# Turning queries and keys by transposing DMA instead of on TensorE, in a kernel of windowed attention and an MLP

## The chip, the cores and the metric

The kernel runs on one core of one Trainium2 chip. The metric is device time in microseconds of one execution; lower is better.

## The reference

Eight batches, eight heads, 576 positions, 64 elements a head. Attention looks at the position itself and the 127 before it, with a bias that falls with distance and has a slope of its own for each head. The heads are put side by side (512 columns), normalised over the columns, and go through two matrix products with a ReLU between them; the input of the normalisation is added to the result.

```python
scores = scale * np.matmul(q, k.transpose(0, 1, 3, 2))
mask = (rel >= 0) & (rel < 128)                 # rel = query position - key position
scores = np.where(mask, scores - slopes * rel, -1e9)
attn = exp(scores - max); attn /= attn.sum(-1)
x = np.matmul(attn, v)                          # heads side by side: (8, 576, 512)
xn = (x - mean) / np.sqrt(var + 1e-6) * g_ln
out = x + np.maximum(xn @ w_ch1, 0.0) @ w_ch2   # 512 -> 2048 -> 512
```

Inputs and outputs are float32; the products run in float16 with float32 sums.

## The kernel before

Batches are taken in four pairs `p` (0 to 3). A pair has nine blocks: blocks 0 to 7 are 128 positions of one batch (block `2i + b` holds positions 128i to 128i + 127 of the pair's batch `b`), and block 8, called `T`, holds the last 64 positions of both batches. `order` lists the 36 blocks; `n` is a block's place in it, so that pairs 2 and 3 are blocks 18 to 35. Blocks are gathered into twelve groups for the MLP, six of two blocks and then six of four.

A block passes through these steps:

- `load_qk` and `load_v` bring q, k and v into SBUF with DMAs from POOL (GpSimd), which turn float32 into float16 on the way. `load_until` issues the loads in the order of `loads`, up to six blocks ahead (`AHEAD`). One `load_qk` serves two blocks (or the tail); its tile is of `raw_pool`, with four buffers for q and four for k, so that a load waits until the turn four before it has read its buffer. Row `c` of a half tile takes positions 2c and 2c + 1, that is 128 neighbouring elements of a head.
- `turn` brings the head's 64 elements onto partitions, as the scores' matmul wants them: 64 transposes of 64 x 64 on TensorE (32 for the tail, line 277) into PSUM, and copies from there to SBUF on VectorE (DVE) and ScalarE (ACT). Where `in_sc` is set they use the two pairs of banks of the scores, `ps_sc`. Queries stay in the order "even positions, then odd ones", keys are put back into natural order by the copy (lines 296 and 297). The tables of `distances`, and from them the masks, have the queries' order. The tiles are of `turned_pool`.
- `attend` (line 393) multiplies queries and keys in 64 x 64 tiles and leaves out, through `seen`, what the mask will make zero anyhow; ScalarE takes the exponential (line 401), VectorE multiplies by the mask (line 412).
- `values` multiplies by v (line 445); VectorE divides by the row sums (lines 453, 454) and so empties the PSUM bank.
- From block 8 on, `stats` makes mean and variance on VectorE (lines 542, 543) and the reciprocal deviation `rstd` with two small operations on POOL (lines 497 and 500). `normal` makes `xc` on VectorE (line 484) and turns it with a transposing DMA on SP (SyncE) into the group's `xT` (line 492).
- `mlp1` (line 677) makes the hidden layer, `mlp2` (line 710) or `fast_mlp2` (line 776, with fewer products) the output. VectorE adds x (`finish`, line 852, or `add`, line 794) and SP stores. In `finish` and `add` a PSUM bank comes free. Products and values share four PSUM banks (`ps_mm`, from the seventh group on as the list `ring`).

For TensorE, ScalarE and VectorE the order of the program is the order written (`manual_schedule`): `steps` holds for each block n the turn of block n + 3, the values of block n, the scores of block n + 2, the statistics and then `normal` of block n, and `weave_at` sets these steps between the matmuls of the MLP. For POOL and SP the order is found by the scheduler when the program is built; each engine works through its list strictly in order. A DMA on SP or POOL waits, beside its data, for the eighth DMA before it on its queue.

A store writes rows back in two DMAs, one for even and one for odd positions, except for the tails.

Of the kernel before, what the change touches and what calls it, by code (L numbers as in the profile page):

```python
# [10 lines left out]
FP16 = mybir.dt.float16  # L11
# [6 lines left out]
P = 128  # L18
# [4 lines left out]
T = 8  # L23
# [2 lines left out]
GROUPS = [2] * 6 + [4] * 6  # L26
FAST = 6

NV = 10
AHEAD = 6  # L30

FIRST_GROUPS, FIRST = 2, 4
# [6 lines left out]
def distances():  # L39

    key = np.arange(P)[:, None]
    query = np.arange(P)[None, :]

    def far(rel, ok=True):
        return np.where(ok & (rel >= 0) & (rel < WINDOW), rel, FAR)

    ends = [far(P + query - HALF * b - key, query // HALF == b) for b in range(2)]  # L50
    tail = far(query - key, query // HALF == key // HALF)
    evens_first = np.r_[0:P:2, 1:P:2]
    both = [far(P + query - key), far(query - key)]
    cols = [m[:, evens_first] for m in both] + [*ends, tail]
    return np.concatenate(cols, axis=1).astype(np.float16)


# [1 line left out]
def kernel(  # L59
# [21 lines left out]
    def pool(name, bufs, **kw):  # L81
        return ctx.enter_context(tc.tile_pool(name=name, bufs=bufs, **kw))

    consts = pool("consts", 1)
    raw_pool = pool("raw", 4)
    turned_pool = pool("turned", 3)
    probs_pool = pool("probs", 4)
    own_pool = pool("own", 2)
    x_pool = pool("x", 7)
# [34 lines left out]

    g_sb = consts.tile([P, NKB], FP32)
    nc.sync.dma_start(out=g_sb, in_=moe_g_ln.rearrange("(kb p) -> p kb", p=P))
    g_line = consts.tile([1, DM], FP32)
    nc.sync.dma_start(out=g_line, in_=moe_g_ln.rearrange("(o d) -> o d", o=1))
    g_row = consts.tile([P, DM], FP32)
    one_line = consts.tile([1, P], FP32)  # L130
    magic = consts.tile([P, 4], I32)
    ones = consts.tile([P, 4 * P], FP16)
# [3 lines left out]
    w1 = consts.tile([P, NKB, FFN], FP16)  # L136
    w1g = consts.tile([P, NKB, FFN], FP16)
    w2 = consts.tile([P, NFB, DM], FP16)
    QF, QD = NFB // 2, DM // 2
    hsum = [consts.tile([P, QF, 2 * P], FP16, name=f"hs{i}", tag=f"hs{i}") for i in range(2)]  # L140
    spare = [w1[:, i, :].rearrange("p (f d) -> p f d", d=QD) for i in range(4)]
    hsum.append(spare[3])
    vext = [
# [60 lines left out]

    raw = {}

    def load_qk(src, tag, p, i):

        n = min(P, S - i * P)
        t = raw_pool.tile([P, H, 2, D], FP16, tag=tag, name=tag)  # L210
        raw[tag, p, i] = t
        for b in range(2):
            nc.gpsimd.dma_start(  # L213
                out=t[b * n // 2 : (b + 1) * n // 2],
                in_=src[2 * p + b, :, i * P : i * P + n, :].rearrange(
                    "h (c r) d -> c h r d", r=2
                ),
            )
# [64 lines left out]
    def turn(p, i, in_sc=False, copies=(nc.vector.tensor_copy, nc.scalar.copy)):  # L283

        ps = [bank(b if in_sc else None) for b in range(2)]
        k = keys_tile("k", p, i)  # L290
        if i < 4:
            q = queries(p, i)
            transposed("q", p, i, [t[:, 0] for t in ps])
            transposed("k", p, i, [t[:, 1] for t in ps])
            for b, copy in enumerate(copies):
                copy(out=q[:, b], in_=ps[b][:, 0])  # L296
                copy(out=k[:, b].rearrange("p h (c r) -> p r h c", r=2), in_=ps[b][:, 1])  # L297
        else:
            q = keys_tile("q", p, i)
            for tag, t, dst, copy in zip("qk", ps, (q, k), copies):  # L300
                transposed(tag, p, i, [t[:, 0]])
                copy(out=dst[:, 0].rearrange("p h (c r) -> p r h c", r=2), in_=t[:, 0])

    def bank(sc=None):
        if sc is None:
            return ps_mm.tile([P, 2, 2, HP, HALF], FP16, tag="mm", name="ps_tr")
        return ps_sc[sc][:, 0].bitcast(FP16).rearrange(
            "p (t r h c) -> p t r h c", t=2, r=2, h=HP
        )

    def queries(p, i):
        t = turned_pool.tile([P, 2, 2, HP, HALF], FP16, tag="q", name="q")
        turned["q", p, i] = t.rearrange("p b r h c -> p b h r c")
        return t

    def keys_tile(tag, p, i):
        t = turned_pool.tile([P, 2, HP, P], FP16, tag=tag, name=tag)
# [2 lines left out]

    def turn_first():

        q, k = queries(0, 0), keys_tile("k", 0, 0)
        ps = [bank(b)[:, 0] for b in range(2)]
        transposed("q", 0, 0, ps)
        for b in range(2):
            nc.vector.tensor_copy(out=q[:, b], in_=ps[b])
        ps_row = spread_g()
        warm(2)
        ps = [bank(b)[:, 0] for b in (0, None)]  # L330
        transposed("k", 0, 0, ps)
        for b, copy in enumerate((nc.scalar.copy, nc.vector.tensor_copy)):
            copy(out=k[:, b].rearrange("p h (c r) -> p r h c", r=2), in_=ps[b])
        nc.vector.tensor_copy(out=g_row, in_=ps_row)
# [11 lines left out]
        return t  # L346

    weights_of, unmasked, scored = {}, {}, []

    def in_halves(t):  # L350
        return t if len(t.shape) == 3 else t.rearrange("p (r c) -> p r c", r=2)

    def seen(p, blk, o, t):


        both, every = slice(0, 2), slice(0, HALF)
        first, second = slice(0, HALF // 2), slice(HALF // 2, HALF)
        if p == 0 and blk < SEEN:
            return [(0, both, every), (1, both, every)]
        if blk == T:  # L360
            batches = [slice(0, 1), slice(1, 2)]
            return [(c, batches[c if o == T else t], every) for c in range(2)]
        if o == blk:
            return [(0, both, every), (1, both, second)]
        return [(1, both, every), (0, both, first)]

    def attend(p, blk, keys, mask, tag, hps):

        heads = slice(2 * hps[0], 2 * hps[-1] + 2)
        nk = len(keys)
        if hps[0] == 0:
            home_pool = own_pool if tag == "own" else probs_pool
            pr = home_pool.tile([P, H, nk, P], FP16, tag=tag, name=tag)
            for t, o in enumerate(keys):
                weights_of.setdefault((p, blk), []).append((pr, t, o))
        else:  # L380
            pr = weights_of[p, blk][-1][0]
        banks = ps_sc[len(scored) % 2]
        scored.append((p, blk))
        ps = banks.rearrange("p j (n t q) -> p j n t q", n=len(hps), t=nk)
        qt, b = turned["q", p, blk // 2], blk % 2
        for n, hp in enumerate(hps):
            for t, o in enumerate(keys):
                kt = turned["k", p, o // 2][:, o % 2]
                for c, r, queries in seen(p, blk, o, t):
                    cols = slice(c * HALF, (c + 1) * HALF)  # L390
                    for j in range(2):
                        rows = slice(j * HALF, (j + 1) * HALF)
                        nc.tensor.matmul(  # L393
                            in_halves(ps[cols, j, n, t, :])[:, r, queries],
                            kt[rows, hp, cols],
                            in_halves(qt[rows, b, hp])[:, r, queries],
                            start=True,
                            stop=True,
                        )
        dst = pr[:, heads].rearrange("p h t q -> p h (t q)")  # L400
# [239 lines left out]
    for n in range(8, count):  # L640
        first_half, second_half = values_steps(n)
        steps.append(
            turn_step(n + 3, True) if n + 3 < count and order[n + 3][1] % 2 == 0 else []
        )
        step = first_half + second_half[:1]
        if n + 1 < count and order[n + 1][1] == T:
            step += [(scores_tail, order[n][0])]
        if n + 2 < count:
            step += scores_step(n + 2)
        steps.append(step)  # L650
        steps.append(
            [m for t in (n + 1, n + 2) if t < count for m in masks_of(t)] + [(stats, n)]
        )
        steps.append([(normal, n)])
# [207 lines left out]
    def store(p, blk, o, cols=slice(0, DM), queues=(nc.sync,)):  # L862
        queues = cycle(queues)
        for b, t0, w, p0 in spans(p, blk):
            dst, src = out[b, t0 : t0 + w, cols], o[p0 : p0 + w, cols]
            if blk == T:
                next(queues).dma_start(out=dst, in_=src)
            else:
                dst = dst.rearrange("(c r) d -> r c d", r=2)
                for r in range(2):  # L870
                    next(queues).dma_start(
                        out=dst[r], in_=src[r * HALF : (r + 1) * HALF]
                    )

    def weave_at(units, *places, also=()):
        for u, _ in enumerate(units):
# [70 lines left out]
```

## Time and the profile before

| What | Value |
|---|---|
| Median of three runs | 322.67 us (322.29 to 323.87) |
| The profiled execution | 322.94 us |
| Its span on the core | 321.1 us |
| TensorE matmuls | 307.5 us busy, 4478 instructions |
| VectorE | 233.4 us busy |
| ScalarE | 184.6 us busy |
| POOL | 114.9 us busy |
| Issue of a transposing DMA on SP (28 of them) | 1.19 us median |

The span runs from the program's first to its last instruction in the profile; the time of an execution has 1.8 us more around it. An engine's busy time leaves out its waits. A "releaser" is the instruction whose semaphore ended a wait. DMA issues on SP and the landing of their data are told apart: an issue occupies the queue, the landing comes later.

### The profile page before, as it was taken

The numbers are of one execution on the slowest core, as the hardware profiler recorded it, in microseconds if no ns is written. First come the engines' busy times: TensorE is split into PE (matmuls) and PEld (weight loads), VectorE is DVE, ScalarE is ACT, GpSimd is POOL, SyncE is SP. The second block draws the span as 40 slices with busy tenths as digits, with TensorE's granted clock in tenths as the row PEclk, the third lists the DMA queues.
The fourth block names the chain that finished last, engine by engine and source line by source line (L and its number), as shares of the span: only waits on it lengthen the run. The fifth ranks groups of instructions, "written<-read, shape, count | busy, mean of one in ns | idle before, by whom it ended". The sixth has DMA issues, their size and how long they took to land.

```text
span 321.1 us, 10472 instructions
## 1 busy us (share of the span) xinstructions
PE 307.5 (96%) x4478; PEld 207.3 (65%) x4478; DVE 233.4 (73%) x556; ACT 184.6 (57%) x320; POOL 114.9 (36%) x188
## 2 busy tenths in 40 slices
PE   8889999999899999999999999999999999999993
PEld 2478655758558576545875587558755874685582
DVE  2788878786687788758994899579958984761462
ACT  6588756666558466478248824873488247405600
POOL 8833657769145264534252534220000001000000
PEclk9999999999999999999999999999999999999999
DMA  9999999999999899895389769660340134015005
GB/s 113 169 206 196 190 142 189 186 115 184 59 118 120 78 143 92 89 160 55 45 108 160 68 68 115 117 51 18 84 85 18 18 68 98 18 32 117 0 2 131
DMA packets 102048, 32.34 MB, mean 101 GB/s; under 512 B 92913, under 2 KB 97649, under 8 KB 102002
## 3 DMA queue, kind: packets, MB, share of 16 engines
q0 software_dynamic: 79872, 18.36, 66.7%
q1 hardware_dynamic: 21810, 13.05, 19.5%
q8 instruction: 35, 0.57, 0.8%
q10 hardware_dynamic: 320, 0.26, 0.4%
q14 instruction: 11, 0.09, 0.1%
HBM read 36.90 MB, written 9.44 MB: 144 GB/s over the span
## 4 chain that ended last, share of the span: by engine, by line
PE 76%; DVE 10%; ACT 5%; POOL 3%; DMA 2%; issue 2%; POOLq 0%; ACTq 0%
PE ps_r L677 24%; PE ps_r L776 21%; PE ps_m L710 10%; PE ps_m L677 9%; PE ps_sc L393 4%; ACT probs L401 3%; PE ps_sc L277 2%; PE ps_r L445 2%; DVE probs L412 2%; DMA k<-in_k_dram 2%; PE ps_pv L445 2%; DVE st L542 1%; POOL rstd L500 1%; POOL q L213 1%; DVE o L852 1%
## 5 line engine op out<-in xcount | busy, mean ns | idle before, releaser
L677 PEld LDWEIGHTS <-w1g 128*128 128x128 f16 x640 | 60.0, 98 | 48.9 <-issue 1.8
L677 PE MATMUL ps_r<-xT,w1g 128*128 128x512 f16 x384 | 85.5, 379 | 0.0
L401 ACT ACTIVATE probs<-ps_sc 128x1024 f16<-128x1024 f32 x56 | 54.3, 1027 | 35.5 <-PE ps_sc L393 35.5
L693 ACT ACTIVATE ht<-ps_r 128x512 f16<-128x512 f32 x96 | 56.2, 600 | 30.6 <-PE ps_r L677 30.4
L497 POOL TENSOR_TENSOR rstd<-moments,powers 128x1 f32<-128x1 f32 x28 | 5.4, 193 | 118.5 <-DVE moments L543 118.4
L710 PE MATMUL ps_m<-w,ht 128*128 128x512 f16 x192 | 46.0, 380 | 0.0
L776 PE MATMUL ps_r<-w,ht 128*128 128x256 f16 x384 | 44.1, 273 | 0.0
L223 POOL DMA_DIRECT2D vx<-in_v_dram x40 | 34.6, 879 | 22.4 <-PE ps_r L445 9.7
L412 DVE TENSOR_TENSOR probs<-probs,m 128x1024 f16<-128x1024 f16 x56 | 37.3, 688 | 6.5 <-ACT probs L401 6.3
L776 PEld LDWEIGHTS <-ht 128*128 128x128 f16 x384 | 37.1, 98 | 4.7
L693 ACT ACTIVATE ht<-ps_m 128x256 f16<-128x256 f32 x91 | 33.1, 388 | 8.6 <-PE ps_m L677 6.0
L213 POOL DMA_DIRECT2D q<-in_q_dram x40 | 27.4, 692 | 14.4 <-PE ps_sc L277 6.6
L677 PE MATMUL ps_m<-xT,w1g 128*128 128x256 f16 x256 | 31.4, 273 | 1.1 <-ACT ht L693 0.8
L213 POOL DMA_DIRECT2D k<-in_k_dram x40 | 26.8, 684 | 6.7 <-DMA w<-in_moe_w_ch_dram 3.1
L710 PEld LDWEIGHTS <-ht 128*128 128x128 f16 x192 | 17.1, 98 | 17.4
L484 DVE TENSOR_SCALAR xc<-x,moments,rstd 128x512 f16<-128x512 f16 x28 | 11.5, 412 | 20.0 <-POOL rstd L500 19.0
L542 DVE BATCH_NORM_STATS2 st<-x 128x6 f32<-128x512 f16 x36 | 24.6, 684 | 0.0
L393 PE MATMUL ps_sc<-q,k 64*64 64x128 f16 (+1 forms) x1088 | 20.2, 208 | 3.9 <-DVE k L297 1.3
L296 ACT COPY q<-ps_sc 128x512 f16<-128x512 f16 x15 | 8.8, 586 | 25.1 <-PE ps_sc L277 24.9
L776 PE MATMUL ps_r<-w,hs 128*128 128x256 f16 x192 | 22.5, 273 | 0.0
L445 PEld LDWEIGHTS <-probs 128*128 128x128 f16 x448 | 18.7, 97 | 4.7 <-DVE probs L412 0.3
L393 PEld LDWEIGHTS <-k 64*64 64x64 f16 x1088 | 15.2, 107 | 8.9 <-issue 6.5
(85 smaller groups left out, 390.7 us busy)
## 6 DMA issues: line engine op xcount, KB each, us to landing
out_dram<-o SPq DMA_DIRECT2D x68, 128.0 KB, 2.5
q<-in_q_dram POOLq DMA_DIRECT2D x32, 128.0 KB, 4.5
k<-in_k_dram POOLq DMA_DIRECT2D x32, 128.0 KB, 5.8
vx<-in_v_dram POOLq DMA_DIRECT2D x32, 128.0 KB, 7.6
w<-in_moe_w_ch_dram POOLq DMA_DIRECT2D x8, 512.0 KB, 12.2
q<-in_q_dram POOLq DMA_DIRECT2D x8, 64.0 KB, 4.8
k<-in_k_dram POOLq DMA_DIRECT2D x8, 64.0 KB, 4.3
vx<-in_v_dram POOLq DMA_DIRECT2D x8, 64.0 KB, 6.0
```

What stands on the lines that cost most here:

```text
L213: nc.gpsimd.dma_start(out=t[b * n // 2 : (b + 1) * n // 2], in_=src[2 * p + b, :, i * P : i * P + n, :].rearrange("h (c r) d -> c h r d", ...
L223: nc.gpsimd.dma_start(out=vx[p0 : p0 + n, :, 0:D], in_=v[b, :, t0 : t0 + n, :].rearrange("h p d -> p h d"),)
L393: nc.tensor.matmul(in_halves(ps[cols, j, n, t, :])[:, r, queries], kt[rows, hp, cols], in_halves(qt[rows, b, hp])[:, r, queries], start=Tr ...
L401: nc.scalar.activation(out=dst.rearrange("p (n j) q -> p j n q", j=2), in_=ps.rearrange("p j n t q -> p j n (t q)"), func=AF.Exp, scale=in ...
L412: nc.vector.tensor_tensor(out=dst, in0=dst, in1=mask, op=ALU.mult)
L445: nc.tensor.matmul(ps[:, i, :], pr[:, h, t, :], vext[(p * NSLOT + o) % NV][:, h, :], start=(n == 0), stop=(n == len(terms) - 1),)
L484: nc.vector.tensor_scalar(out=xc, in0=xs[order[n]], scalar1=moments[:, n, 0:1], scalar2=rstd[:, n : n + 1], op0=ALU.subtract, op1=ALU.mult,)
L542: nc.vector.bn_stats(out=st, in_=xs[order[n]])
L677: nc.tensor.matmul(ps[:, 0:cols], w[:, kb, fb * P : (fb + 1) * P], xT[:, kb, 0:cols], start=(kb == 0), stop=(kb == NKB - 1),)
L693: nc.scalar.activation(out=ht[:, fb, 0:cols], in_=ps[:, 0:cols], func=AF.Relu)
L710: nc.tensor.matmul(sums[at], ht[:, fb, at * P : (at + 1) * P], w2[:, fb, :], start=(fb == 0), stop=(fb == NFB - 1),)
L776: nc.tensor.matmul(banks[name][pair][:, pair, :], lhs[:, fb, pair * P : (pair + 1) * P], rhs[:, fb, :], start=(first and fb == 0 and (pair ...
```

## The change

For pairs 2 and 3 (the last 18 blocks, ten turns) q and k are loaded in natural order, 64 elements of a head to a row, and turned by DMAs on SP: `dma_start_transpose` from the raw tile straight into the turned tile, four for a turn (q and k of two batches), two for a tail. These turns stand one block earlier in `steps` (block n + 4). Turned tiles get four buffers instead of three. Queries of all blocks are now in natural order, so that the copies of pairs 0 and 1 write queries as they write keys, the masks' columns are not reordered, and a block's output goes out in one DMA. After a turn has used the scores' banks, the next scores in each of them are computed whole (`junk`). The two tables of `g` lie in the space of the hidden layer's sums.

```diff
+NV, RAW = 10, 4
+BY_DMA_TURN = 2
...
-    cols = [m[:, evens_first] for m in both] + [*ends, tail]
+    cols = [*both, *ends, tail]
...
-    turned_pool = pool("turned", 3)
+    turned_pool = pool("turned", 4)
...
+    def by_dma(p):
+        return p >= BY_DMA_TURN
...
+        if by_dma(p):
+            t = raw[tag, p, i] = t.rearrange("p h r d -> p (h r d)").rearrange(
+                "p (b h d) -> p b h d", b=2, h=H
+            )
         for b in range(2):
+            if by_dma(p):
+                nc.gpsimd.dma_start(
+                    out=t[:, b] if i < 4 else t[b * n : (b + 1) * n, 0],
+                    in_=src[2 * p + b, :, i * P : i * P + n, :].rearrange(
+                        "h p d -> p h d"
+                    ),
+                )
+                continue
...
+        q, k = (keys_tile(tag, p, i) for tag in "qk")
+        if by_dma(p):
+            for tag, dst in (("q", q), ("k", k)):
+                src = raw.pop((tag, p, i))
+                for b in range(2 if i < 4 else 1):
+                    nc.sync.dma_start_transpose(
+                        out=dst[:, b], in_=src[:, b].rearrange("p h d -> p (h d)")
+                    )
+            return
...
-                copy(out=q[:, b], in_=ps[b][:, 0])
-                copy(out=k[:, b].rearrange("p h (c r) -> p r h c", r=2), in_=ps[b][:, 1])
+                for t, dst in enumerate((q, k)):
+                    copy(
+                        out=dst[:, b].rearrange("p h (c r) -> p r h c", r=2),
+                        in_=ps[b][:, t],
+                    )
...
+        junk[sc] = True
...
-        if p == 0 and blk < SEEN:
+        if junk[len(scored) % 2] or p == 0 and blk < SEEN:
             return [(0, both, every), (1, both, every)]
...
-            turn_step(n + 3, True) if n + 3 < count and order[n + 3][1] % 2 == 0 else []
+            [
+                f
+                for m in (n + 3, n + 4)
+                if m < count and order[m][1] % 2 == 0 and by_dma(order[m][0]) == (m == n + 4)
+                for f in turn_step(m, True)
+            ]
...
-            if blk == T:
-                next(queues).dma_start(out=dst, in_=src)
-            else:
-                dst = dst.rearrange("(c r) d -> r c d", r=2)
-                for r in range(2):
-                    next(queues).dma_start(
-                        out=dst[r], in_=src[r * HALF : (r + 1) * HALF]
-                    )
+            next(queues).dma_start(out=dst, in_=src)
```

More of the change, by code (lines that the diff above doesn't have):

```diff
@@ L27 @@
 FAST = 6
-NV = 10
+NV, RAW = 10, 4
+BY_DMA_TURN = 2
 AHEAD = 6
@@ L51, in distances @@
     tail = far(query - key, query // HALF == key // HALF)
-    evens_first = np.r_[0:P:2, 1:P:2]
     both = [far(P + query - key), far(query - key)]
-    cols = [m[:, evens_first] for m in both] + [*ends, tail]
+    cols = [*both, *ends, tail]
     return np.concatenate(cols, axis=1).astype(np.float16)
@@ L84 @@
     consts = pool("consts", 1)
-    raw_pool = pool("raw", 4)
-    turned_pool = pool("turned", 3)
+    raw_pool = pool("raw", RAW)
+    turned_pool = pool("turned", 4)
     probs_pool = pool("probs", 4)
@@ L126 @@
     nc.sync.dma_start(out=g_sb, in_=moe_g_ln.rearrange("(kb p) -> p kb", p=P))
-    g_line = consts.tile([1, DM], FP32)
+    QF, QD = NFB // 2, DM // 2
+    hsum = [consts.tile([P, QF, 2 * P], FP16, name=f"hs{i}", tag=f"hs{i}") for i in range(2)]
+    g_line, g_row = (
+        t.rearrange("p f d -> p (f d)")[:, 0 : 2 * DM].bitcast(FP32) for t in hsum
+    )
+    g_line = g_line[0:1]
     nc.sync.dma_start(out=g_line, in_=moe_g_ln.rearrange("(o d) -> o d", o=1))
-    g_row = consts.tile([P, DM], FP32)
     one_line = consts.tile([1, P], FP32)
@@ L138 @@
     w2 = consts.tile([P, NFB, DM], FP16)
-    QF, QD = NFB // 2, DM // 2
-    hsum = [consts.tile([P, QF, 2 * P], FP16, name=f"hs{i}", tag=f"hs{i}") for i in range(2)]
     spare = [w1[:, i, :].rearrange("p (f d) -> p f d", d=QD) for i in range(4)]
@@ L283, in turn @@
     def turn(p, i, in_sc=False, copies=(nc.vector.tensor_copy, nc.scalar.copy)):
+        q, k = (keys_tile(tag, p, i) for tag in "qk")
[7 more added lines that the diff above has]
+            return
         ps = [bank(b if in_sc else None) for b in range(2)]
-        k = keys_tile("k", p, i)
         if i < 4:
-            q = queries(p, i)
             transposed("q", p, i, [t[:, 0] for t in ps])
@@ L295, in turn @@
             for b, copy in enumerate(copies):
-                copy(out=q[:, b], in_=ps[b][:, 0])
-                copy(out=k[:, b].rearrange("p h (c r) -> p r h c", r=2), in_=ps[b][:, 1])
+                for t, dst in enumerate((q, k)):
+                    copy(
+                        out=dst[:, b].rearrange("p h (c r) -> p r h c", r=2),
+                        in_=ps[b][:, t],
+                    )
         else:
-            q = keys_tile("q", p, i)
             for tag, t, dst, copy in zip("qk", ps, (q, k), copies):
@@ L309, in bank @@
         )
[L311 to L314, printed above, removed]
     def keys_tile(tag, p, i):
@@ L321, in turn_first @@
     def turn_first():
-        q, k = queries(0, 0), keys_tile("k", 0, 0)
+        q, k = (keys_tile(tag, 0, 0) for tag in "qk")
         ps = [bank(b)[:, 0] for b in range(2)]
@@ L326, in turn_first @@
         for b in range(2):
-            nc.vector.tensor_copy(out=q[:, b], in_=ps[b])
+            nc.vector.tensor_copy(
+                out=q[:, b].rearrange("p h (c r) -> p r h c", r=2), in_=ps[b]
+            )
         ps_row = spread_g()
@@ L348 @@
     weights_of, unmasked, scored = {}, {}, []
+    junk = [False, False]
     def in_halves(t):
@@ L356, in seen @@
         both, every = slice(0, 2), slice(0, HALF)
-        first, second = slice(0, HALF // 2), slice(HALF // 2, HALF)
-        if p == 0 and blk < SEEN:
+        if junk[len(scored) % 2] or p == 0 and blk < SEEN:
             return [(0, both, every), (1, both, every)]
@@ L363, in seen @@
         if o == blk:
-            return [(0, both, every), (1, both, second)]
-        return [(1, both, every), (0, both, first)]
+            return [(0, both, every), (1, slice(1, 2), every)]
+        return [(1, both, every), (0, slice(0, 1), every)]
     def attend(p, blk, keys, mask, tag, hps):
@@ L382, in attend @@
         banks = ps_sc[len(scored) % 2]
-        scored.append((p, blk))
         ps = banks.rearrange("p j (n t q) -> p j n t q", n=len(hps), t=nk)
@@ L399, in attend @@
                         )
+        junk[len(scored) % 2] = False
+        scored.append((p, blk))
         dst = pr[:, heads].rearrange("p h t q -> p h (t q)")
```

## The prediction

> **What bounds the kernel now.** First the page's busy line, the TensorE clock row and the chain by engine:
>
> ```profile
> PE 307.5 (96%) x4478; PEld 207.3 (65%) x4478; DVE 233.4 (73%) x556; ACT 184.6 (57%) x320; POOL 114.9 (36%) x188
> PEclk9999999999999999999999999999999999999999
> PE 76%; DVE 10%; ACT 5%; POOL 3%; DMA 2%; issue 2%; POOLq 0%; ACTq 0%
> ```
>
> TensorE bounds the span at full clock; only 14 us of 321.1 are without a matmul. The 10% of DVE and 3% of POOL say that in places VectorE and the small POOL operations are the path. The table of stretches places that (columns: stretch, length, busy us of PE, PEld, DVE, ACT, POOL, clock, DMA share, GB/s):
>
> ```profile
> 115.00:135.00 20.00, 19.07 (x360) 12.79 (x358) 16.37 (x39) 12.65 (x26) 9.68 (x17) 1.00 1.06 114
> 135.00:160.00 25.00, 24.62 (x324) 15.75 (x323) 19.70 (x44) 15.60 (x24) 9.47 (x17) 1.00 1.00 88
> 200.00:255.00 55.00, 54.87 (x789) 36.75 (x788) 43.48 (x93) 33.72 (x51) 7.53 (x17) 1.00 0.35 56
> ```
>
> From 115 to 135 us DVE is at 82% and TensorE still finds 0.9 us of waits; after 200 us TensorE waits for nothing. Third, the timeline around one turn that the change removes, and around the one large wait in 115 to 135 us (start, length, group):
>
> ```profile
> 147.17 0.81 PE L677 MATMUL ps_r<-xT,w1g 128*128 128x512 f16 x3
> 147.91 0.45 PE L277 MATMUL ps_sc<-iden,q 64*64 64x64 f16 x32
> 148.18 0.44 PE L277 MATMUL ps_sc<-iden,k 64*64 64x64 f16 x32
> 148.55 0.82 PE L677 MATMUL ps_r<-xT,w1g 128*128 128x512 f16 x3
> ...
> 121.57 0.32 PE L393 MATMUL ps_sc<-q,k 64*64 64x64 f16 x16 [0.67 <-DVE k L297]
> ```
>
> A turn holds TensorE from 147.91 to 148.55: 0.64 us. Fourth, the line of the existing transposing DMAs on SP (min/median/max ns of issue, then us to landing), and POOL and DVE at step 17:
>
> ```profile
> L492 SPq DMA_TRANSPOSE xT<-xc x28: 1189/1196/2362, 80.8 to 283.6; - x28
> DMA to landing us min/median/max: 2.4/3.6/7.5
> ...
> 135.72 3.17 POOL L223 DMA_DIRECT2D vx<-in_v_dram  x4
> 138.85 0.25 POOL L497 TENSOR_TENSOR rstd<-moments,powers 128x1 f32<-128x1 f32 x1
> 139.18 0.56 POOL L500 TENSOR_TENSOR rstd<-rstd,powers 128x1 f32<-128x1 f32 x1
> 139.78 0.41 DVE L484 TENSOR_SCALAR xc<-x,moments,rstd 128x512 f16<-128x512 f16 x1 [1.63 <-POOL rstd L500]
> ```
>
> A transposing DMA holds SP 1.19 us, and the data are there 2.4 us after the issue at best. And rstd stands in POOL's queue behind loads: here four v loads made it late, and VectorE, strictly in order, stood 1.63 us at xc.
>
> **What is removed.** Ten turns (eight of 64 transposes, two of 32 that take 0.69 us each instead of 0.71): 10 x 0.64 = 6.4 us of TensorE. With them go scores' waits for their copies: 0.67 us at 121.57, 0.38 at 166.63, 0.13 at 223.79, and 0.38 at 151.09 (for a reciprocal that had stood behind a turn's copies): 1.5 us. The copies themselves (eight times 0.42 + 0.72 us on DVE and 0.59 + 0.74 on ACT, and 0.72 + 0.73 twice) lie beside matmuls and count nothing more. Sum: -7.9 us.
>
> **What is added in front of 113 us.** Queries of the first two batch pairs are now copied with a two-element stride, as keys are: 0.72 instead of 0.42 us on DVE, 0.74 instead of 0.59 on ACT, some nine times. Mostly beside matmuls; where ACT is the path (14 to 19 us) two ACT copies cost 0.3 us. After each turn that overwrites the scores' banks, the next two halves are computed whole: four turns, so eight halves; a run of 32 scores matmuls (two halves) takes 0.64 us whole (at 41.5 us) and 0.54 cut (at 93.6), so 8 x 0.05 = 0.4 us. Outputs in one DMA instead of two free 32 x 0.59 us of SP; SP is idle most of the time there: nothing. The tables' place: nothing. Sum: +0.6 us (0 to 1.2).
>
> **Loads in natural order.** A row of a q or k load is now 64 elements, as in v's loads: 0.91 us of POOL (v's median) instead of 0.69, 36 loads by 0.2 to 0.25 = 8 us of a POOL that is 36% busy; and 18,432 more packets. The page's queue line gives 66.7% of 16 engines' 321.1 us for 79,872 packets, 43 ns each, so 18,432 x 43 ns / 16 = 49 us more of mean engine time, from 74 to 200 us, where the DMA share is already about 1. Off the path, since a load is issued about six blocks (50 us) ahead and lands in 5.2 us; but it keeps landing times high.
>
> **The transposing DMAs and what they queue behind.** 36 more, 36 x 1.19 = 43 us on SP, on average no load. What counts is the order of the built program. I number blocks n from 0, step n being block n's values, and write T(2,0) for the turn of blocks 18 and 19, and so on. SP: xT13; T(2,0) (4 DMAs); a store; T(2,2) (4); q of T(2,4) (2); xT14; k of T(2,4) (2); xT15; T(2,6) (4); a store; xT16; a store; q of T(2,8) (1); xT17. POOL: the raw buffers are four deep, and a load now waits until the *landing* of the turn four before it. The order is: q and k of (2,8), behind T(2,0); **in their midst rstd14**; (3,0) and q of (3,2); first k load of (3,2), behind k of T(2,4); **rstd15**; first q load of (3,4), behind T(2,6); **rstd16**; first q load of (3,6), behind T(2,8); **rstd17**. In the kernel before, the same loads waited for TensorE's transposes alone. So a loop forms: rstd -> xc -> xT on SP -> turns on SP -> landing -> load on POOL -> next rstd. Walked with times of the trace, 1.19 us an issue, and a landing of 4.0 us (alone 2.4; the four xT between 119 and 141 us took 5.2, 2.4, 6.0, 4.9; a turn's DMAs follow each other and loads are in flight):
> - xT13 is issued at 113.5. T(2,0) runs 114.8 to 119.6, its last lands at 122.4. POOL: load 0.7, rstd 0.19, load 0.7, pow 0.56: xc14 at 124.5 (before 119.5).
> - VectorE stands; values of block 15 are drained at 126.7 instead of 122.6. The product pool has four banks, two held by these values, so the third L677 unit behind them waits: TensorE 4.0 us later than before, T(2,0)'s gain already inside.
> - SP goes on issuing to 127.4, then xT14, k of T(2,4) at 128.6 and 129.8, landing 133.8; load 0.93, rstd, load 0.93, pow: xc15 at 136.4 (before 126.8). Then 4.4 us of DVE work as in the trace until the output of block 10 frees its bank: 140.8, where TensorE's values at 133.7 wait: 7.1 us later.
> - xT15 136.8, q of T(2,6) 138.0 and 139.2, landing 143.2; load, rstd, load, pow: xc16 at 145.8 (132.1). Block 11's output follows at 146.8; the second L677 unit of the next group, at 135.8 before, needs that bank: **TensorE 11.0 us later**.
> - xT16 146.2, a store, q of T(2,8) 148.0, landing 152: xc17 at 154.2, its values' bank is needed at 156.3 and free at 155.8. The loop is caught up.
> - At step 19, k of T(2,8) and q of T(3,0) are released by scores; three issues, a landing and two loads make xc19 about 2.3 us late; DVE is dense there, I take half: 1.2.
> Later turns stand at least four steps (31 us) ahead of their scores and in front of an rstd whose moments come later: nothing.
>
> Sum: 11.0 (in it the first two turns and the 0.67 us) + 1.2 - 8 x 0.64 - 0.9 + 0.6 = +6.8 us. The profiled execution took 322.94 us (321.1 span; the median of three is 322.67): 329.7. With a landing of 2.4 the loop's xc16 comes 3.2 us earlier and step 19 costs 0.3: 325.7; with 6.0, 4 us later, xc17 1.5 us late in its turn and step 19 1 us more: 336.3.
>
> The Trainium skill, "DMA: Bandwidth & Descriptors", section "Issuing engines are not separate DMA queues", holds the time to initiate a DMA as usually small against the DMA itself. The row differs: 1.19 us of issue of 2.4 to landing. The trace has no two transposing DMAs back to back, so that the second's issue could be hidden stays possible; that is the first rival.
>
> **Rivals.** (1) *Faster: the loop does not close.* If following transposes are issued much quicker than 1.19 us (decides at about 0.5 us: T(2,0) then lands by 119, and ten of them pass in 5 us), rstd14 is not late and only the gain is left: 322.94 - 7.9 + 0.6 = 315.6. For: SP is nearly idle, the turns have 31 us of lead. Against: 1189 ns is the minimum of 28. By the skill's rule it would come out so. (2) *Only the first link bites*: TensorE loses 5.3 us at block 15 and the banks then hold out: 315.6 + 5.3 = 320.9. Against: xc15 is late by SP's issues alone. (3) *Transfers*: doubled packets and 36 transposes keep landing at 6 to 7.5 us all along, each of four links pays it: 337 to 341. For: DMA share 1.06; against: the loads themselves stand still while POOL waits. That TensorE keeps the turns is ruled out by the built program: 576 matmuls fewer.
>
> **How the numbers follow.** Forecast 0.70 (325 to 337), rival 1 0.18, rival 2 0.07, rival 3 0.05. The range takes in the forecast's own, rival 2 and the upper edge of a partly working rival 1: 317 to 337. About 0.5% (1.6 us) is what a measurement of this kernel tells from no change: faster takes rival 1 and a little of 2, slower the forecast and rival 3: 0.21, 0.06, 0.73.
>
> **What would show it.** Right: no L277-like transposes after 115 us; "DVE xc <- POOL rstd" rising from 19 us to over 30, most of it from 119 to 155 us, POOL waiting there for landings of SP's transposes, PE idle some 15 us between 121 and 148 us, and 200 to 255 us about 2 us shorter in work. Wrong: following transposes issued under 0.6 us apart, rstd14 to rstd17 less than 1 us behind their moments, PE without gaps there (rival 1); landings above 6 us with POOL waiting for its own loads (rival 3).

## The result and the profile after

The changed kernel takes **348.35 us** (346.03 to 348.95), the kernel before 323.04 us on the same chip: ratio 1.077, 95% interval 1.071 to 1.083. Forecast were 329.7 us and a range of 317 to 337: slower, as forecast, but by 25 us and not by 7. The profiled execution took 348.95 us, its span is 347.2 us.

The page after: busy line, TensorE's busy tenths and clock in 40 slices of 8.7 us, the chain by engine.

```profile
PE 308.5 (89%) x3902; PEld 204.9 (59%) x3902; DVE 224.9 (65%) x538; ACT 175.6 (51%) x302; POOL 122.0 (35%) x188
PE   8889999998899906739595999999999999999994
PEclk9999999999999976967899899999999999999998
PE 67%; DMA 11%; DVE 6%; POOL 5%; ACT 5%; issue 3%; SPq 0%; POOLq 0%; ACTq 0%
```

576 matmuls are gone, and yet TensorE is busy 1.0 us longer than before (307.5). From the 15th slice (121 us) to the 22nd it stands in places, and the granted clock, full in all slices before, falls there too, or in the slice behind. DMA has risen from 2% of the chain to 11%. The table by stretches (columns as in the prediction) gives the place:

```profile
115.00:135.00 20.00, 8.99 (x134) 6.81 (x134) 8.69 (x21) 8.00 (x17) 10.00 (x14) 0.78 1.66 149
135.00:160.00 25.00, 17.35 (x146) 8.46 (x145) 9.12 (x23) 6.12 (x10) 13.60 (x19) 0.77 1.53 124
160.00:195.00 35.00, 27.14 (x270) 17.52 (x269) 19.00 (x41) 13.44 (x20) 8.83 (x15) 0.90 0.91 70
195.00:260.00 65.00, 65.00 (x790) 45.21 (x789) 50.60 (x111) 34.28 (x49) 14.31 (x27) 1.00 0.76 109
```

Nearly all is lost between 115 and 195 us; from there on TensorE waits for nothing, as before. The first stand can be followed through four timelines (start, length, group, and in brackets the idle time before it and its releaser). SP, where the transposes of turns are issued; POOL; VectorE; TensorE:

```profile
114.92 1.27 SPq L517 DMA_TRANSPOSE xT<-xc  x1
116.35 3.11 SPq L311 DMA_TRANSPOSE q<-q  x2
119.63 2.55 SPq L311 DMA_TRANSPOSE k<-k  x2
```
```profile
127.29 1.38 POOL L223 DMA_DIRECT2D q<-in_q_dram  x2 [9.19 <-DMA q<-q]
128.64 0.71 POOL L223 DMA_DIRECT2D k<-in_k_dram  x1
129.33 0.23 POOL L522 TENSOR_TENSOR rstd<-moments,powers 128x1 f32<-128x1 f32 x1
129.46 0.72 POOL L223 DMA_DIRECT2D k<-in_k_dram  x1
130.18 0.58 POOL L525 TENSOR_TENSOR rstd<-rstd,powers 128x1 f32<-128x1 f32 x1
```
```profile
119.47 0.18 DVE L568 BATCH_NORM_AGGREGATE moments<-st 128x2 f32<-128x6 f32 x1
130.80 0.41 DVE L509 TENSOR_SCALAR xc<-x,moments,rstd 128x512 f16<-128x512 f16 x1 [11.14 <-POOL rstd L525]
```
```profile
121.28 1.05 PE L707 MATMUL ps_m<-xT,w1g 128*128 128x256 f16 x8
133.02 3.38 PE L707 MATMUL ps_m<-xT,w1g 128*128 128x256 f16 x15 [10.70 <-DVE x L479]
```

T(2,0) is issued from 116.35 to 122.18 us; its four transposes land at 123.57, 126.74, 127.15 and 127.60 us, 6.6 to 9.0 us after their issue. POOL stands 9.2 us at a load whose raw buffer the second of them still reads, with rstd14 behind it. Block 14's moments are ready at 119.65; rstd14 comes at 130.76. VectorE stands 11.1 us at xc14, block 15's values stay in their bank, and TensorE stands 10.7 us. This is the chain that the prediction wrote down, link for link; only the landing that released POOL was that of the second q (126.74 us), where the prediction let the last of k decide. In the sums over the span (engine and line, waited for: us, times, longest):

```profile
DVE xc L509 <- POOL rstd L525: 57.0, 24, 11.1
POOL q L223 <- DMA q<-q: 26.9, 5, 9.2
POOL k L223 <- DMA k<-k: 13.2, 3, 7.2
```

The first was 19.0 us before; the two others didn't exist. TensorE's stands of over 1 us, each with the time at which it ended: 10.70 us to 133.02, 1.30 to 146.28, 2.62 to 151.22, 2.82 to 155.91, 3.81 to 170.64, 4.04 to 190.43. All its gaps after 100 us make 26.8 us.

The clock is the second part. The table, cut where the granted clock changes:

```profile
122.40:126.16 3.76, 0.00 (x0) 0.00 (x0) 0.00 (x0) 1.43 (x3) 0.00 (x0) 1.00 1.82 109
126.16:136.40 10.24, 3.38 (x16) 2.41 (x17) 5.23 (x12) 1.15 (x3) 7.91 (x11) 0.50 1.59 172
136.40:147.80 11.40, 9.19 (x101) 4.84 (x99) 2.47 (x7) 2.71 (x4) 5.16 (x7) 1.00 1.63 112
150.06:160.30 10.24, 6.26 (x15) 2.20 (x16) 4.00 (x10) 1.79 (x3) 7.43 (x10) 0.50 1.36 129
```

3.8 us into the stand the clock falls to half, and it stays there until 3.4 us after TensorE has begun again. In 150 to 160 us fifteen matmuls take 6.26 us, 0.42 each. Two more stretches of 0.5, of 3.41 us, follow (from 170.54 and 191.02).

### The profile page after: what moved, and what is told of

It is laid out like the page before. It is cut to its first block, busy times and chain, and to the rows that moved or that the text cites. A ratio compares the mean times of both kernels' runs of the same rounds, so it can differ in the third digit from the quotient of the medians.

```text
span 347.2 us, 9307 instructions
## 1 busy us (share of the span) xinstructions
PE 308.5 (89%) x3902; PEld 204.9 (59%) x3902; DVE 224.9 (65%) x538; ACT 175.6 (51%) x302; POOL 122.0 (35%) x188
## 4 chain that ended last, share of the span: by engine, by line
PE 67%; DMA 11%; DVE 6%; POOL 5%; ACT 5%; issue 3%; SPq 0%; POOLq 0%; ACTq 0%
PE ps_r L707 23%; PE ps_r L806 20%; PE ps_m L707 8%; DMA q<-q 8%; PE ps_m L740 7%; PE ps_sc L416 3%; ACT probs L426 2%; PE ps_r L470 2%; DMA k<-k 2%; DMA k<-in_k_dram 2%; PE ps_pv L470 2%; POOL q L223 2%; POOL rstd L525 1%; PE ps_sc L294 1%; DVE x L479 1%
## 5 line engine op out<-in xcount | busy, mean ns | idle before, releaser
L707 PEld LDWEIGHTS <-w1g 128*128 128x128 f16 x640 | 62.5, 101 | 74.2 <-issue 17.5
L707 PE MATMUL ps_r<-xT,w1g 128*128 128x512 f16 x384 | 89.7, 394 | 9.3 <-DVE x L479 3.8
L707 PE MATMUL ps_m<-xT,w1g 128*128 128x256 f16 x256 | 32.9, 282 | 11.7 <-DVE x L479 10.7
L223 POOL DMA_DIRECT2D q<-in_q_dram x20 | 17.2, 865 | 28.8 <-DMA q<-q 26.9
L223 POOL DMA_DIRECT2D k<-in_k_dram x20 | 17.1, 862 | 14.1 <-DMA k<-k 13.2
L806 PEld LDWEIGHTS <-hs 128*128 128x128 f16 x192 | 18.8, 98 | 2.2
```

Of the source, the lines that this page charges most:

```text
L223: nc.gpsimd.dma_start(out=t[:, b] if i < 4 else t[b * n : (b + 1) * n, 0], in_=src[2 * p + b, :, i * P : i * P + n, :].rearrange("h p d -> ...
L707: nc.tensor.matmul(ps[:, 0:cols], w[:, kb, fb * P : (fb + 1) * P], xT[:, kb, 0:cols], start=(kb == 0), stop=(kb == NKB - 1),)
L806: nc.tensor.matmul(banks[name][pair][:, pair, :], lhs[:, fb, pair * P : (pair + 1) * P], rhs[:, fb, :], start=(first and fb == 0 and (pair ...
```

## The experiments

Each was timed in several rounds beside the kernel before on the same chip, whose medians were 322.7 to 323.7 us; ratios are to that. The numbering of blocks and turns is the prediction's.

**Theory:** the loop through POOL's and SP's order is the whole loss, and the turns in themselves gain. **Rivals:** the rest of the change loses; the transposes' and loads' transfers lose (rival 3 of the prediction); SP's order alone loses.

**1. The rest of the change alone.**

```diff
-BY_DMA_TURN = 2
+BY_DMA_TURN = 4
```

> All 36 blocks are turned on TensorE again; everything else of the change stays (queries in natural order, strided query copies, one output DMA a block, whole scores after a turn, tables moved, four turned buffers). Theory (the loop POOL - SP - POOL makes the loss): in the changed kernel the 13th block's transposing DMA, ahead of the first turn by DMA, was already 1.4 us later than before, so 1.4 us for pairs 0 and 1 and as much again at most for pairs 2 and 3: 323 to 326 us. Rival (the layout itself costs, by slower copies, whole scores or one large store): over 330 us.

Measured: 325.65 us (324.98 to 327.56), ratio 1.008 (1.005 to 1.011), clock 1.00, no gap over 0.8 us after 100 us. Queries in natural order, one store a block, and scores computed whole cost 3.0 us when all 36 blocks pay it. They are not the loss.

**2. The order of POOL, of SP, and of both, written by hand.** `manual_schedule` leaves the listed engines in the order in which the program writes their instructions. A load, which the scheduler had put ahead of a ready rstd, then stands where `load_until` calls it, in the step of a block's values, behind earlier blocks' rstd.

```diff
-    with tc.manual_schedule(engines={engine.PE}):
+    with tc.manual_schedule(engines={engine.PE, engine.Pool}):             # e_pool
+    with tc.manual_schedule(engines={engine.PE, engine.SP}):               # e_sp
+    with tc.manual_schedule(engines={engine.PE, engine.Pool, engine.SP}):  # e_both
```

POOL alone:

> The changed kernel with POOL's list in the written order: rstd of block n stands ahead of the loads of block n + 7 and behind loads whose buffers came free long ago; SP's list is again found by the scheduler. Theory (rstd waits on POOL behind loads that wait for turns' landings): VectorE's wait for rstd falls from 57 us to about 20 us, TensorE's gaps between 120 and 195 us from 27 us to under 4 us, and the time to 316 to 319 us (323.0 + 1.5 in front - 7.9 for ten turns). Rival S (the blocks' own transposes stand behind turns on SP, 1.3 us each): no more than half of the loss goes, over 330 us. Rival T (landing times of 5 to 9 us from doubled load packets): over 330 us as well, with TensorE waiting for turned tiles.

SP alone:

> The changed kernel with SP's list in the written order (a turn's four DMAs at the start of the step, four blocks ahead of their use, never ten in a row); POOL's list is found by the scheduler and still has loads of k, which wait for turns, ahead of rstd. Theory: the loop is still there, with shorter passes because a landing waits for four issues and not for ten: 325 to 345 us, VectorE's wait for rstd over 30 us. Rival S: with no row of ten turns ahead of the blocks' own transposes the loss is gone, under 320 us.

Both:

> The changed kernel with POOL's and SP's lists both in the written order. Theory: neither queue makes rstd late, 315 to 318 us, no gap of TensorE over 1 us between 115 and 300 us, clock at 1.0. Rival T (transfers): landings of turns and blocks' transposes still 4 to 7 us between 75 and 200 us, and over 323 us.

Measured: POOL alone 320.09 us (319.43 to 321.82), ratio 0.990 (0.984 to 0.995), 1.1 us above its bracket. SP alone 349.54 us (347.48 to 350.07), ratio 1.079 (1.073 to 1.085): the expectation missed, the order on SP by itself gives nothing, since rstd still stands behind the landings and VectorE still waits 49.1 us for it. Both: **314.07 us** (313.64 to 316.50), ratio 0.972 (0.966 to 0.978), a little below its bracket. With POOL alone one stand is left. It ends as an xT lands that SP issued behind a turn (issued at 129.91, landed at 138.44); the row's own releaser, an xc, ends at the same moment:

```profile
138.57 7.65 PE L707 MATMUL ps_r<-xT,w1g 128*128 128x512 f16 x23 [4.34 <-DVE xc L509]
```

With both lists, the page's busy line and the same stretches:

```profile
PE 300.0 (96%) x3902; PEld 201.9 (65%) x3902; DVE 226.1 (72%) x538; ACT 175.2 (56%) x302; POOL 123.4 (39%) x188
```
```profile
115.00:135.00 20.00, 19.07 (x243) 12.47 (x239) 15.77 (x39) 12.06 (x24) 10.85 (x16) 1.00 2.11 137
135.00:160.00 25.00, 25.00 (x277) 16.70 (x275) 19.84 (x43) 14.88 (x22) 12.05 (x18) 1.00 1.47 134
```

The same matmuls take 300.0 us instead of 308.5, all gaps after 100 us make 1.6 us instead of 26.8, and VectorE's wait at xc is 18.0 us. In this kernel the transposes land hardly sooner (three of T(2,0)'s 6.2, 7.2 and 7.5 us after issue, the later ones up to 190 us 3.6 to 9.1), and the DMA share from 115 to 135 us is higher; that costs nothing visible. So slow landings by themselves lose nothing; what stood in order behind them did.

**3. Control: the kernel before with both lists in the written order.** The same edit, in the kernel before.

> Control: the kernel before with POOL's and SP's lists in the written order, nothing else. If the order of the lists matters only where loads wait for turns by DMA: 321 to 326 us, as the kernel before. If the written order alone is what made the changed kernel with both lists fast (314 us): under 318 us.

Measured: 322.68 us (322.31 to 323.55), ratio 0.998 (0.996 to 1.000). The written order in itself is worth nothing here; what the kernel with both lists gains belongs to the change.

**4. The wider rows back.** The natural order doubles the packets of q and k of pairs 2 and 3.

```diff
-            if by_dma(p):
+            if by_dma(p) and i == 4:
...
+            if by_dma(p):
+                rows = slice(b * n // 2, (b + 1) * n // 2)
+                nc.gpsimd.dma_start(
+                    out=whole[rows],
+                    in_=src[2 * p + b, :, i * P : i * P + n, :].rearrange(
+                        "h (c r) d -> c h r d", r=2
...
```

> The changed kernel with the same lists on every engine, but the full q and k tiles of pairs 2 and 3 are loaded in rows of 128 elements as before (half the packets, 0.69 instead of 0.9 us of POOL); positions of two batches come to lie in each other's place, so the scores are of other rows, and the amount of work is the same. Theory: the loop is in the lists; with fewer packets in front of them the first turns land after 5 to 6 us instead of 7 to 9, each pass is 2 us shorter: 336 to 345 us. Rival T (the doubled packets are what makes the loss): under 330 us.

Measured: 344.45 us (340.93 to 348.28), ratio 1.061 (1.054 to 1.068). The doubled packets account for some 4 of the 25 us (the medians differ by 3.9; single runs of the two kernels overlap). T(2,0) still lands 6.1 to 7.6 us after issue, and the chain is the same, with a first stand of 9.1 us.

**5. Only pair 3 turned by DMA.** This leaves one link: the load of the last tail, which waits for T(3,0). In the changed kernel it stands ahead of rstd19, and the prediction priced it at 1.2 us (step 19); here it stands ahead of rstd23.

```diff
-BY_DMA_TURN = 2
+BY_DMA_TURN = 3
```

> Only pair 3 (five turns) by DMA, lists found by the scheduler. The raw buffers are four deep, so of all loads only those of the last tail wait for a turn by DMA. Theory: no loop; 325.7 (all turns on TensorE) less 5 x 0.64 and up to 1 us of scores' waits: 321 to 323 us. Rivals S and T (turns on SP, doubled packets): they would take half of what the ten turns lose, 335 us and more.

Measured: 327.66 us (326.98 to 329.17), ratio 1.014 (1.010 to 1.018): a miss. Only one pair of loads still waits for a turn's landing (the raw buffers of the last turns), at 188 to 199 us, and once more rstd stands behind it. POOL, then TensorE:

```profile
192.29 1.38 POOL L223 DMA_DIRECT2D q<-in_q_dram  x2 [4.20 <-DMA q<-q]
197.50 1.36 POOL L223 DMA_DIRECT2D k<-in_k_dram  x2 [3.84 <-DMA k<-k]
198.86 0.22 POOL L522 TENSOR_TENSOR rstd<-moments,powers 128x1 f32<-128x1 f32 x1
```
```profile
200.82 2.50 PE L806 MATMUL ps_r<-w,w 128*128 128x256 f16 x11 [6.40 <-DVE o L824]
```

One link of the loop, without any other, costs a stand of 6.4 us and a stretch of half clock (6.83 us long, from 197.63, inside the stand). The gain of these turns doesn't pay for that.

**6. A stand by other means.** In the kernel with both lists (314.07 us) VectorE gets sixteen additions of 0.7 us ahead of xc14, in place of the 11-us wait. No instruction waits for a turn's landing. Does the clock fall all the same?

```diff
+        steps.append(([(stand,)] if n == 14 else []) + [(normal, n)])   # stand: 16 tensor_tensor, 128 x 1024
```

> The kernel with both lists in the written order (314.1 us) and, ahead of xc of block 14, sixteen extra VectorE additions of 0.68 us into unused space: one stand of 10.9 us where the changed kernel's first one is, nothing else. If a stand costs TensorE only its length: 323 to 325 us, clock 1.0. If TensorE's granted clock falls after a stand, as the changed kernel's rows have it from 121 to 208 us: 326 to 331 us, mean clock under 0.99.

Measured: 322.93 us (322.35 to 324.52), ratio 1.000 (0.997 to 1.002): 8.9 us over the kernel it is made from. VectorE, then the clock:

```profile
119.72 11.56 DVE L521 TENSOR_TENSOR hs<-w 128x1024 f16<-128x1024 f16 x16
131.20 0.41 DVE L509 TENSOR_SCALAR xc<-x,moments,rstd 128x512 f16<-128x512 f16 x1
```
```profile
19.02:22.43 3.41, 3.41 (x32) 2.66 (x29) 1.78 (x6) 1.63 (x3) 0.50 (x2) 0.50 1.24 207
131.66:138.49 6.83, 5.08 (x49) 2.42 (x50) 5.74 (x15) 1.94 (x2) 1.80 (x4) 0.50 0.11 22
```

The total lies just under both brackets, because they took the stand for longer than it became: TensorE's gaps grew by 5.5 us, not by 9 to 11. But the parts separate: 5.5 us of gaps, and matmuls that are busy 3.9 us longer (303.9 against 300.0) for the same instructions. Not all of the 3.9 belongs to the stand. The trace has a stretch of half clock at 19.02 us too, ahead of the additions, as the kernel with the wider rows has at 19.48 and no other. By half of the busy time in each stretch, the stand is worth some 2.5 us (5.08 us busy) and the one at 19 us 1.7 us (3.41 us busy). Behind the stand the clock is half with a DMA share of 0.11, so the fall needs neither transposes nor a busy DMA.

**7. rstd off POOL.** The loop cut at another place: nine small operations on VectorE (`inv_std`; the expectation of the control below counts seven) make rstd; the landings stay where they are.

```diff
     def stats(n):
         variance(n)
-        here = rstd[:, n : n + 1]
...
+        inv_std(n, 1)
```

> The changed kernel with the reciprocal deviation of blocks 8 to 35 made on VectorE (nine small operations of about 0.17 us for a block, as blocks 0 to 7 have them) instead of on POOL; loads still wait on POOL for landings of turns, and SP's list still has rows of turns. Theory: the loop's link from POOL to VectorE is cut; what is left is the loss on SP (about 6 us between the kernels with one and with both lists in the written order) and 28 x 1.5 us more of VectorE, of which some lies where VectorE is the path: 318 to 328 us. If instead late loads or landings by themselves hold TensorE up: over 335 us.

Measured: 340.08 us (339.15 to 342.73), ratio 1.052 (1.046 to 1.057): a miss by 12 us. VectorE no longer waits at xc, the stand of 10.7 us is gone, though POOL still waits 35.7 us for turns' landings; but TensorE waits 0.4 to 1.4 us at a time for VectorE's outputs as far as 300 us. One longer stand, 5.0 us to 142.74, ends as an xT lands (142.64) that SP had issued at 134.43. Are the many short waits VectorE's extra work? Two controls, the kernel before and the kernel with both lists, each with rstd on VectorE:

> The kernel before, with rstd made on VectorE (seven small operations a block instead of two on POOL). Control for the changed kernel with rstd on VectorE, which took 340.1 us. If what was left there is the extra VectorE work (37 us of small operations, VectorE 78% busy, TensorE waiting 0.4 to 1.4 us for its outputs up to 300 us), this kernel, with VectorE going from 233 to about 270 us, loses as well: 332 to 342 us. If what was left is still the turns' landings on POOL and SP, this kernel hardly loses: 322 to 327 us.

> The changed kernel with POOL and SP in the written order (314.1 us) and rstd made on VectorE too. No loop here in either case. If the extra VectorE work is what costs, it loses as much as the kernel before does from the same edit, 10 to 20 us: 324 to 334 us. If the turns' landings were what was left in the changed kernel with rstd on VectorE, it loses little: 314 to 319 us.

Measured: the kernel before **340.40 us** (339.78 to 342.38), ratio 1.054 (1.048 to 1.061); with both lists 333.33 us (333.13 to 333.81), ratio 1.031 (1.027 to 1.035). The control's page, busy line and chain:

```profile
PE 310.3 (92%) x4478; PEld 209.0 (62%) x4478; DVE 270.4 (80%) x808; ACT 185.5 (55%) x320; POOL 93.1 (28%) x132
PE 46%; DVE 38%; issue 4%; DMA 4%; ACT 3%; POOL 3%; DVEq 0%; ACTq 0%; POOLq 0%
```

The small operations cost 17 us in the kernel before (323.39 to 340.40) and 19.3 us with both lists (314.07 to 333.33). This explains the miss, if the costs add: of the 26.0 us by which the changed kernel with rstd on VectorE stays behind 314.07, 19.3 are VectorE's work and 6.7 are what the landings on POOL and SP's order still cost. With rstd behind the landings the same difference is 34.3 us (348.35 to 314.07). So some four fifths of the loss are rstd's place in POOL's queue; POOL's order alone gives back as much (348.35 to 320.09, 28.3 us).

**8. Further along the way the experiments point.** Both lists in the written order, and pair 1 turned by DMA as well (15 turns); the second condition places the first of these turns that falls before the loop of `steps`.

```diff
-BY_DMA_TURN = 2
+BY_DMA_TURN = 1
...
-                if ... by_dma(order[m][0]) == (m == n + 4)
+                if ... by_dma(order[m][0]) == (m == n + 4 or n == 8)
...
+    with tc.manual_schedule(engines={engine.PE, engine.Pool, engine.SP}):
```

> Both lists in the written order, and pair 1 is turned by DMA as well (15 turns instead of ten). Theory: five more turns of 0.64 us and their copies leave the three engines: 309 to 313 us. Against it: pair 1 is loaded while the weights' loads hold the DMA engines, from 45 to 100 us; if landings decide there, TensorE waits for turned tiles before 110 us and the time is over 316 us.

Measured: **310.48 us** (309.76 to 313.37), ratio 0.959 (0.954 to 0.965). This beats both kernels; TensorE is busy 294.5 us, 96% of the span, at full clock, with 1.7 us of gaps after 100 us.

## Why the prediction was right, and where it was not

**Right: the mechanism.** rstd14 to rstd17 stand in POOL's queue behind loads that wait for landings; VectorE stands at xc; values keep their banks; TensorE stands from 121 us on. Of what was to show it right, most came: the wait at xc rose to 57.0 us (over 30 forecast), POOL waited for landings of SP's transposes, TensorE stood 12.9 us from 121 to 148 (some 15 forecast), and from xT24 to xT31 the kernel takes 1.6 us less than before (about 2). But not most of the 57.0 us lies between 119 and 155 us: 25.7 do, and 21.5 follow up to 200. Writing POOL's order alone takes the time from 348 to 320 us, which no rival explains.

**Right, in part by luck: the gain.** Without the loop the prediction had 315.6 us; the kernel without the loop runs at 314.07. The parts came otherwise: TensorE's busy time fell by 7.5 us (307.5 to 300.0), where 6.4 less 0.4 were forecast; its gaps after 100 us fell by 0.7 us (2.3 to 1.6), where 1.5 were.

**Wrong: the sum, by 19.3 us** (span 347.2 against 327.9 forecast: 329.7 less 1.8), and with it the range. Against the kernel with both lists, whose span is 312.7, the trace has 34.5 us more: 25.2 of gaps (26.8 less 1.6), 8.5 of longer matmuls (308.5 less 300.0), 0.8 of the rest. The prediction had 14.1 us of gaps in all (11.0 and 1.2, and the two turns and the 0.67 us that it put inside the 11.0), and none of longer matmuls. The rest of the 19.3 is small: the 0.8, the gains, which came out 1.1 us better, and 1.0 us of little gaps that the kernel with both lists has and the changed kernel lacks. Three terms failed:

- *The clock, 8.5 us, was no term at all.* The prediction read the full clock of the kernel before as a given and carried it through a forecast in which TensorE stands for 5 us and more. The profile of before could have told of it only at its end, where TensorE has nothing left to do. The Trainium skill, "TensorE: Matmul & The Clock Gate", section "What's actually happening", does: by it the clock goes to half after at least one idle window of about 3.4 us, and back after about as long of activity. The traces agree on the lengths: in every kernel here the stretches of half clock before the end are 3.41, 6.83 or 10.24 us long. Each kernel with a stand over 4 us has some, the kernel with both lists has none, and experiment 6 makes one with VectorE's work alone. The traces don't bear out that the stretch ahead of a fall must be idle: in 17 of 22 falls TensorE had been busy for 0.2 to 1.97 of the last 3.41 us, and the control of experiment 7, the kernel before with rstd on VectorE, has a fall behind a stand of 1.57 us.
- *"A landing of 4.0 us" and what follows it: 5.4 us of gaps up to 156 us (18.4 against 13.0).* The first turn landed 6.6 to 9.0 us after issue, with five loads issued between 113.6 and 118.1 us still under way. xc14 came at 130.8 and not 124.5, 6.3 us later. The prediction let the last landing (122.4) release POOL; in the trace the second q's did, at 126.74, 9.0 us after its issue and 4.3 later than that. The other 2.0 us arose mostly because four loads stood between this landing and pow where two were counted. The further landings that released a load ahead of an rstd took 7.2 (rstd15), 3.3 (rstd16), 8.6 (rstd17) and 5.5 us (rstd19). The row of landings that was at hand (2.4, 3.6, 7.5) held such values; the four xT's beside the 4.0 have a mean of 4.6, and no other transposes beside them. Even the prediction's upper case, 6.0, lay below all four of the first turn.
- *"The loop is caught up" at xc17, and the 1.2 us of step 19: 6.7 us (7.9 against 1.2).* The loop wasn't caught up. The q of T(2,8) was issued at 157.29 and landed at 165.93; the load that waited for it stands ahead of rstd17, and xc17 came at 169.02 and not 154.2. POOL, VectorE, TensorE:

```profile
166.46 0.88 POOL L223 DMA_DIRECT2D q<-in_q_dram  x1 [6.71 <-DMA q<-q]
167.36 0.21 POOL L522 TENSOR_TENSOR rstd<-moments,powers 128x1 f32<-128x1 f32 x1
169.02 0.41 DVE L509 TENSOR_SCALAR xc<-x,moments,rstd 128x512 f16<-128x512 f16 x1 [10.07 <-POOL rstd L525]
170.64 6.96 PE L707 MATMUL ps_r<-xT,w1g 128*128 128x512 f16 x24 [3.81 <-DVE x L479]
```

  The stand of 4.0 us to 190.43 is step 19's, behind q of T(3,0), at 1.2 in the sum; experiment 5, with that link alone, has 6.4. The turns still later cost nothing, as the prediction said: from 195 to 260 us TensorE is busy 65.00 of 65.00 us.

A small one: the front cost 1.4 us (xT13 at 114.92 instead of 113.54), not 0.6, a little above its bound of 1.2; experiment 1 shows it for all blocks.

**The rivals.** (1) The loop doesn't close because following transposes are issued quickly: no. They mostly follow each other by 1.3 to 1.4 us, each holding SP about as long as one alone. By the rule that the prediction took from the Trainium skill ("DMA: Bandwidth & Descriptors", section "Issuing engines are not separate DMA queues") initiating is usually small against the DMA itself; here an issue of 1.2 us stands against 2.4 us to landing at best and 6.6 to 9.0 in the first turn. (2) Only the first link bites: no, five stands follow. (3) Transfers: the price came nearest (337 to 341), and part of it came true: four of the five landings above took over 5 us, and the links of the loop paid for them. But doubled packets are not what makes them so long, since the wider rows give back 4 us only, and without the order behind them long landings cost nothing, as the kernel with both lists shows.

What stays open: why a landing takes 7 us there and 2.4 at best. Loads in flight go with it: in the 14 traces, after 60 us, the median transpose lands after 2.4 us where no load is under way or issued within 2 us, whether other transposes are under way or not, and after 5.3 us (alone) to 7.4 us (beside other transposes) where four or more loads are. That is read from the traces, and no run isolated it; the wider rows, with half the packets, left T(2,0) at 6.1 to 7.6.

## What to carry to other kernels

When work moves to a DMA, list what stands in order behind each instruction that will now wait for its landing, on every queue; a 0.2-us operation behind it can be worth more than all that was moved (here 34 us against a gain of 9). Where a scheduler orders the queues, write the order by hand for those on which waits for landings meet small operations of the critical path, and run that order in the old kernel too, to know whose the gain is. When a forecast contains stands of TensorE, count matmuls at half clock behind them: here each kernel with a stand of over 4 us had some, and so had two with none over 1.9 us (the controls of experiment 7).

## What the runs showed of the hardware that was not expected

- TensorE's granted clock is halved in stretches of 3.41 us or two or three times that, and not by idle time alone. The falls of one trace lie whole multiples of 3.41 us apart. Cut into pieces of 3.41 us by its falls, each of the 14 traces says the same: all 22 falls before the end follow a piece in which TensorE was busy for at most 1.97 us, and no piece with less than 1.57 us was spared. The fall at 150.06 us, for instance, follows 3.41 us with 1.18 us of matmuls. Full clock came back after pieces with at least 3.3 us of matmuls; after 2.4 us or less it stayed at half. Price here: 8.5 us for the four stretches of the changed kernel, some 2.5 for the one that experiment 6 made.
- Transposing DMAs of 128 x 512 float16 issued back to back on SP are issued no faster than single ones: most hold SP for 1.2 to 1.3 us each, some for up to 2.5 us, which was not explained. They land after 2.4 us at best, also in a row (the two k of T(2,6), issued at 149.73 and 151.03, as the last of the loads came in), and mostly after 5 to 9 us with four or more loads in flight; 4 us was no fair middle.
- The doubled packets took less than forecast: POOL's queue was worth 66.7% of 16 engines' 321.1 us before, and

```profile
q0 software_dynamic: 98304, 18.36, 72.6%
```

of 347.2 us now, which is 38 us more of mean engine time for 18,432 more packets, not 49.
